# One PSUM bank, one more product in halves and two steps of delay in a gated mix of linear attention and a GEGLU network

## The chip, the cores and the metric

The kernel runs on one core of a Trainium2 chip. Its engines work beside each other and are kept in order by semaphores: TensorE (PE in the profile; its weight loads are PEld), VectorE (DVE), ScalarE (ACT), GpSimd (POOL) and SyncE (SP), whose queue issues most transfers. Matmuls write to PSUM, which has 8 banks of 512 float32 columns for each of 128 partitions. The metric is the device time of one execution in microseconds, as the median of several runs.

## The reference

The input x has 2048 tokens of 640 features (bfloat16). Two branches are computed from it and mixed by a gate for each token.

```python
def _A_ref(x, wqkv, w_phi, wo):          # linear attention, 32 heads of 20
    q, k, v = ...(x @ wqkv)
    pq = einsum("bhsd,hdf->bhsf", q, w_phi); pk = einsum("bhsd,hdf->bhsf", k, w_phi)
    phi_q = concatenate([softmax(pq), softmax(-pq)], axis=-1)
    phi_k = concatenate([softmax(pk), softmax(-pk)], axis=-1)
    kv = einsum("bhsf,bhsd->bhfd", phi_k, v); z = einsum("bhsf->bhf", phi_k)
    num = einsum("bhqf,bhfd->bhqd", phi_q, kv)
    den = einsum("bhqf,bhf->bhq", phi_q, z)[..., None] + 1e-6
    return (num / den) ... @ wo
def _B_ref(x, w_gate, w_up, w_down):     # F = 1728
    return (gelu(x @ w_gate) * (x @ w_up)) @ w_down
g = sigmoid((x * gate_w).sum(-1, keepdims=True))
out = g * _A_ref(x, ...) + (1 - g) * _B_ref(x, ...)
```

## The kernel before

Tokens are worked in 16 tiles of 128 and in 4 batches of 512. The order of all instructions is written out by hand. A small scheduler (`_Sched`) notes for each buffer key, such as a PSUM bank `("ps", b)`, who wrote and who read it last, and gives each new instruction the waits that follow. Every engine runs its instructions in that order, so an instruction that waits holds up all behind it on its engine.

The stages follow each other. `attention_state` (to about 81 us) projects keys, queries and values, takes exponentials on ScalarE, normalizes the key features on VectorE (`k_norm`, lines 617, 625 and 626) and sums the state tile by tile (`gram`, line 637). Then `ffn` runs. First come gate and up of the four batches, with 14 chunks of F columns each, in the order 0, 1, 13, 2, 3, ... 12. Then comes the down phase, one for each batch.

`gateup` (line 760) makes one chunk: 5 matmuls for the gate into the first bank of a pair, 5 for up into the second (line 464). ScalarE takes the gelu from the first bank (line 800), VectorE multiplies it with the second bank (line 803), in `gateup_evac`. The pairs take turns: banks (0, 1) and (6, 7) in batches 0 to 2, (2, 3) and (4, 5) in the first six chunks of batch 3. So chunks 0, 13 and 3 share a pair. Chunk 13 has only 64 gate and 64 up columns; both halves lie in one bank (`bk`), with 5 matmuls in all, one gelu (line 784) and two products (line 789). For chunks 2 to 6 of batch 0 the up half was computed ahead and lies in SBUF (`upheld`); there the pair is turned round, and the gate goes to what is otherwise the second bank. In batch 0 the last four tiles of the state (`gram(12)` to `gram(15)`) come after the first four chunks, and then `kv_state` and `gates` on VectorE.

The last eight chunks of batch 3 are made in groups of two by `gateup_halves` (line 806). It splits each matmul into two of 64 rows that run beside each other, one for a gate bank and one for an up bank (line 818). The groups hold chunks 5 and 6, 7 and 8, 9 and 10, 11 and 12, and use the banks (2, 3) and (4, 5), then twice (0, 1) and (6, 7), then (2, 3) and (4, 5). Before the first group stands numerator 0 in banks 0, 1, 6 and 7, before the third numerator 1 in banks 2 to 5. In the second group, chunk 7 is emptied in halves of 256 columns (`n=2` in `gateup_evac`: gelu of the first half, its product, gelu of the second half, its product), chunk 8 whole.

A numerator (`num`) is a set of 22 small matmuls (line 850) followed by eleven steps on VectorE (lines 868 to 881) and a transposing transfer on SP's queue into `goT` (line 884). In the down phase `down_pair` makes two token tiles at a time from `hT`, `goT` and the down and output weights (line 908), in banks 0, 1, 4 and 5; a batch has 148 steps of two matmuls, and after the steps listed in `at` comes a numerator for a later tile, always in banks 2, 3, 6 and 7. So each numerator waits until VectorE has read the one before out of these banks (line 879).

Of the kernel before, what the change touches and what calls it, by code (L numbers as in the profile page):

```python
# [107 lines left out]
class _Kernel:  # L108
# [651 lines left out]
    def gateup(self, b, c, banks):  # L760
        sc = self.sc
        xs = lambda kt: self.xT[:, kt, b * self.BT:(b + 1) * self.BT]
        xr = [("xT", t) for t in range(4 * b, 4 * b + 4)]
        old = (self.oldw, self.oldk, self.oldq, [("xT", t) for t in range(12)])[b]
        hT, hk = self.hT(b, c), b
        slot = self.gn % 3
        self.gn += 1
        if c < 13:
            i = 0 if c < 7 else 1
            early = c in self.UP + self.LATE  # L770
            done = early and b == 0
            if done:
                banks = banks[::-1]
            for w, wk, bk in ((self.wg_sb, "wg", banks[0]), (self.wu_sb, "wu", banks[1]))[:1 if done else 2]:
                for kt in range(self.KD):
                    key = self.upheld(c)[1] if early and wk == "wu" else (wk, i, kt)
                    self.mm(bk, 0, 512, w[:, kt, c * P:(c + 1) * P], xs(kt), kt == 0, kt == self.KD - 1, xr + [key])
            up, upk = (self.upheld(c)[0], ("upf", c)) if done else (self.bank(banks[1]), ("ps", banks[1]))
            self.gateup_evac(b, c, banks[0], slot, up, upk, old)
        else:  # L780
            bk = banks[0]
            for kt in range(self.KD):
                self.mm(bk, 0, 512, self.wgu_sb[:, kt, :], xs(kt), kt == 0, kt == self.KD - 1, xr + ["wgu0", "wgu1"])
            sc.op("act", lambda e: e.activation(self.gl[64:128, slot, :], self.ps[0:64, bk * 512:bk * 512 + 512],
                                                AF.Gelu_apprx_tanh),
                  reads=[("ps", bk)], writes=[("gl", slot)], guard=self.oldw)
            for r in (0, 1):
                odd = lambda v: v.rearrange("p (u r q) -> p u r q", r=2, q=P)[:, :, r, :]
                sc.op("dve", lambda e: e.tensor_tensor(
                    odd(hT[64 * r:64 * r + 64, :]), odd(self.ps[64:128, bk * 512:bk * 512 + 512]),  # L790
                    odd(self.gl[64:128, slot, :]), ALU.mult),
                    reads=[("ps", bk), ("gl", slot)], writes=[("hT", hk, c, r)], guard=old)
# [13 lines left out]
    def gateup_halves(self, b, cs, pairs, split):  # L806

        sc, KD = self.sc, self.KD
        old = [("xT", t) for t in range(12)]
        for close in (0, 1):  # L810
            for c, banks in zip(cs, pairs):
                i = 0 if c < 7 else 1
                for kt in range(KD):
                    for r in (0, 1):
                        w, wk, bk = ((self.wg_sb, "wg", banks[0]), (self.wu_sb, "wu", banks[1]))[r ^ close]
                        key = self.upheld(c)[1] if c in self.UP + self.LATE and wk == "wu" else (wk, i, kt)
                        a, end = 64 * r, kt == KD - 1
                        sc.op("pe", lambda e: e.matmul(  # L818
                            self.bank(bk), w[a:a + 64, kt, c * P:(c + 1) * P],
                            self.xT[a:a + 64, kt, b * self.BT:(b + 1) * self.BT], start=close == 0 and kt == 0,  # L820
                            stop=close == 1 and end, skip_group_check=True),
                            reads=[("xT", t) for t in range(4 * b, 4 * b + 4)] + [key],
                            writes=[("ps", bk)] + ([("turn", bk)] if end else []), signal=end,
                            after=[("turn", bk)] if close and kt == 0 else ())
                if close:
                    slot = self.gn % 3
                    self.gn += 1
                    self.gateup_evac(b, c, banks[0], slot, self.bank(banks[1]), ("ps", banks[1]), old,
                                     2 if split and c == cs[0] else 1)

    def before_num(self):
        return ([("upf", c) for c in self.UP + self.LATE] + ["kstage", "qstage"] + [("wref", k, h) for k in (0, 3) for h in (0, self.HM)] + [("wref", k, 0) for k in (1, 2, 4)] + [("xtok", k) for k in range(4)] + ["wkT", "wqT"])
# [125 lines left out]
    def ffn(self):  # L958
        self.gn = 0
        self.pn = 0  # L960
        pairs = [(0, 1), (6, 7)]

        order = [0, 1, 13] + list(range(2, 13))

        def gateups(b, after):
            for idx, c in enumerate(order):
                self.gateup(b, c, pairs[self.pn % 2])
                self.pn += 1
                after(idx)

        def downs(b, side):
            p = [(0, 1), (4, 5)]
            n = 0
            for t in (4 * b, 4 * b + 2):
                final = t + 2 == self.NT
                for _ in self.down_pair(t, p + [(2, 3)] if final else p, (256, 256, 128) if final else (320, 320)):
                    n += 1
                    if n in side:
                        self.num(side[n])

        def state(idx):
            if idx < 4:
                self.gram(12 + idx)
            if idx == 3:
                self.kv_state()
                self.gates()

        def none(idx):
            pass

        def last_gateups(b):
            middle, n = [(2, 3), (4, 5)], 6
            for idx in range(n):
                self.gateup(b, order[idx], middle[idx % 2])
            self.num(0, (0, 6))
            for g, banks in enumerate((middle, pairs, pairs, middle)):
                if g == 2:
                    self.num(1, (2, 4))
                self.gateup_halves(b, order[n + 2 * g:n + 2 * g + 2], banks, g == 1)
        at = [(5, 35, 65, 95)] + [(1, 31, 61, 91)] * 3  # L1000
        gateups(0, state)
        gateups(1, none)
        gateups(2, none)
        last_gateups(3)
        for b in range(self.NB):
            downs(b, {at[b][k]: 4 * b + 2 + k for k in range(4 if b < 3 else 2)})
# [44 lines left out]
```

## Time and profile before

| | |
|---|---|
| median of 3 runs | 283.40 us (283.25 to 283.69) |
| the profiled execution | 283.51 us, span 282.2 us |
| TensorE busy | 278.1 us (99% of the span) |
| VectorE, ScalarE busy | 173.3 us, 106.0 us |
| matmuls, weight loads | 2994, 3006 |
| batch 0 of gate and up begins | about 81 us |
| last batch's split groups | 176.84 to about 194.6 us |
| down phases | from about 194.3 us to the end |

The profile is one execution. Its rows give start and duration of instructions or of merged runs of them, what an engine was idle for, and which instruction released it. The chain is followed back from the last instruction, at each step to what released it.

### The profile page before, as it was taken

How to read it: one execution, taken by the hardware profiler on the slowest of the kernel's cores; microseconds unless marked ns; L12 is line 12 of the kernel's file. 1: busy time of each engine (PE TensorE's matmuls, PEld its weight loads, DVE VectorE, ACT ScalarE, POOL GpSimd, SP SyncE). 2: the span in 40 equal slices, each digit the busy share in tenths (PEclk: the TensorE clock that was granted, in tenths of full speed). 3: DMA queues.
4: the chain of work that ended last, by engine and by line, in shares of the span. 5: the costliest groups of instructions: out<-in, count | busy, mean ns of one | idle time of the engine just before them, and what ended most of it. 6: DMA issues, size and time to landing. Idle time of an engine off the chain costs nothing.

```text
span 282.2 us, 7054 instructions
## 1 busy us (share of the span) xinstructions
PE 278.1 (99%) x2994; PEld 186.2 (66%) x3006; DVE 173.3 (61%) x330; ACT 106.0 (38%) x205; POOL 15.1 (5%) x69
## 2 busy tenths in 40 slices
PE   8999999999999999999999999999999999999997
PEld 4576766666665444444444444456999999999996
DVE  2466999999997523333242233866984883883801
ACT  3347977877784332322323223122112112112011
POOL 7511001101000000000000000000000000000000
DMA  7999069787899910000000000101135132242221
GB/s 220 210 227 183 11 135 163 165 168 145 156 187 267 346 50 0 2 0 0 0 3 0 0 0 2 23 2 26 26 46 104 42 73 56 63 60 64 71 74 46
DMA packets 60378, 24.11 MB, mean 85 GB/s; under 512 B 51002, under 2 KB 59834, under 8 KB 60346
## 3 DMA queue, kind: packets, MB, share of 16 engines
q1 hardware_dynamic: 59680, 23.63, 39.1%
q8 instruction: 23, 0.38, 0.6%
q10 hardware_dynamic: 666, 0.03, 0.2%
q14 instruction: 9, 0.07, 0.1%
HBM read 9.04 MB, written 2.62 MB: 41 GB/s over the span
## 4 chain that ended last, share of the span: by engine, by line
PE 97%; DMA 1%; issue 0%; SPq 0%; ACT 0%
PE ps L464 52%; PE ps L908 29%; PE ps L818 6%; PE ps L599 4%; PE ps L478 2%; PE ps L850 2%; PE ps L637 2%; DMA xtok<-in_A_x_dram 1%; PE ps L404 1%; PE ps L342 0%; SPq L230 0%; ACT outsb L921 0%; PE ps L370 0%
## 5 line engine op out<-in xcount | busy, mean ns | idle before, releaser
L800 ACT ACTIVATE gl<-ps 128x512 bf16<-128x512 f32 (+1 forms) x53 | 31.1, 589 | 71.6 <-PE ps L464 57.0
L464 PE MATMUL ps<-xT,wu_sb 128*128 128x512 bf16 x214 | 52.9, 379 | 0.3
L464 PE MATMUL ps<-xT,wg_sb 128*128 128x512 bf16 x214 | 52.7, 379 | 0.3
L464 PE MATMUL ps<-w,xT 128*128 128x362 bf16 (+5 forms) x340 | 51.4, 302 | 0.0
L803 DVE TENSOR_TENSOR hT<-ps,gl 128x512 bf16<-128x512 f32 x34 | 23.4, 691 | 44.3 <-PE ps L464 44.3
L908 PE MATMUL ps<-wd_sb,hT 64*128 64x320 bf16 x648 | 49.5, 296 | 0.0
L908 PEld LDWEIGHTS ps<-wd_sb,hT 64*128 64x128 bf16 x648 | 40.8, 94 | 2.4
L464 PEld LDWEIGHTS ps<-w,xT 128*128 128x128 bf16 x340 | 31.9, 97 | 14.8
L921 ACT ACTIVATE outsb<-ps,Gm 128x320 bf16<-128x320 f32 (+2 forms) x31 | 14.5, 515 | 70.6 <-PE ps L908 70.6
L464 PEld LDWEIGHTS ps<-xT,wu_sb 128*128 128x128 bf16 x220 | 21.5, 98 | 25.6
L464 PEld LDWEIGHTS ps<-xT,wg_sb 128*128 128x128 bf16 x220 | 21.1, 98 | 25.4 <-ACT gl L800 0.4
L908 PE MATMUL ps<-wo_sb,goT 64*128 64x320 bf16 (+2 forms) x340 | 27.5, 288 | 0.0
L617 DVE TENSOR_REDUCE Dk<-Ek 128x66 f32<-128x1320 bf16 x16 | 24.3, 1521 | 2.3 <-ACT gcol L528 2.3
L626 DVE TENSOR_TENSOR Ek<-Ek,Dk 128x1320 bf16<-128x1320 bf16 x16 | 24.5, 1533 | 0.5
L879 DVE TENSOR_TENSOR O<-ps,RH 128x640 bf16<-128x640 f32 x32 | 24.8, 817 | 0.0
L538 ACT ACTIVATE Ek<-ps 128x627 bf16<-128x627 f32 x32 | 20.5, 693 | 6.4 <-PE ps L599 4.9
L538 ACT ACTIVATE Eqt<-ps 128x627 bf16<-128x627 f32 x32 | 20.6, 705 | 2.5 <-PE ps L464 2.5
L908 PEld LDWEIGHTS ps<-wo_sb,goT 64*128 64x128 bf16 x340 | 20.6, 94 | 1.0
L818 PE MATMUL ps<-xT,wg_sb 64*128 64x512 bf16 x80 | 17.7, 376 | 0.0
L818 PE MATMUL ps<-xT,wu_sb 64*128 64x512 bf16 x80 | 17.5, 376 | 0.0
L908 PE MATMUL ps<-wd_sb,xT 64*128 64x320 bf16 (+2 forms) x270 | 16.3, 269 | 0.0
L803 DVE TENSOR_TENSOR xT<-ps,gl 128x512 bf16<-128x512 f32 (+1 forms) x14 | 8.9, 651 | 11.9 <-PE ps L464 6.4
(94 smaller groups left out, 221.1 us busy)
## 6 DMA issues: line engine op xcount, KB each, us to landing
out_dram<-outsb SPq DMA_DIRECT2D x7, 320.0 KB, 3.2
wd_sb<-in_B_w_down_dram SPq DMA_DIRECT2D x1, 2080.0 KB, 10.9
wg_sb<-in_B_w_gate_dram SPq DMA_DIRECT2D x5, 224.0 KB, 3.1
wg_sb<-in_B_w_gate_dram SPq DMA_DIRECT2D x5, 192.0 KB, 3.1
wu_sb<-in_B_w_up_dram SPq DMA_DIRECT2D x5, 192.0 KB, 3.7
wo_sb<-in_A_wo_dram SPq DMA_DIRECT2D x1, 800.0 KB, 9.6
xtok<-in_A_x_dram SPq DMA_DIRECT2D x2, 320.0 KB, 3.3
w<-in_A_wqkv_dram SPq DMA_DIRECT2D x4, 160.0 KB, 3.6
```

The lines of the kernel that those rows point to most:

```text
L464: self.sc.op("pe", lambda e: e.matmul(self.ps[:, bank * 512 + c0:bank * 512 + c0 + n], lhs, rhs, start=first, stop=fin), reads=reads, writ ...
L478: sc.op("pe", lambda e, c0=c0, n=n, bk=bk, col=col: e.matmul(self.bank(bk)[:, col:col + n], self.xT[:, kt, t * P:(t + 1) * P], self.w3[:, ...
L538: self.sc.op("act", lambda e: e.activation(dst, src, AF.Exp, scale=scale), reads=[("ps", b), ("ps", b + 1)], writes=[(name, sl, s)])
L599: self.sc.op("pe", lambda e: e.matmul(out, self.xT[:, kt, t * P:(t + 1) * P], self.w3[:, kt, c:c + 2 * n].rearrange("p (r w) -> p r w", w= ...
L617: self.sc.op("dve", lambda e: e.tensor_reduce(self.Dk[:, se, 0, :].rearrange("p (u h) -> p u h", h=self.HG), self.k_view(se), AX.X, ALU.ad ...
L626: sc.op("dve", lambda e: e.tensor_tensor(v, v, R.rearrange("p (u h) -> p u h", h=self.HG).unsqueeze(3).to_broadcast([P, 2 * self.G, self.H ...
L800: sc.op("act", lambda e: e.activation(self.gl[:, slot, a:a + w], self.bank(bank)[:, a:a + w], AF.Gelu_apprx_tanh), reads=[("ps", bank)], w ...
L803: sc.op("dve", lambda e: e.tensor_tensor(hT[:, a:a + w], up[:, a:a + w], self.gl[:, slot, a:a + w], ALU.mult), reads=[upk, glk], writes=[( ...
L818: sc.op("pe", lambda e: e.matmul(self.bank(bk), w[a:a + 64, kt, c * P:(c + 1) * P], self.xT[a:a + 64, kt, b * self.BT:(b + 1) * self.BT], ...
L879: dve(lambda e, o=o, f=f, s=s: e.tensor_tensor(o, V[s][:, :, 0:DH], f, ALU.mult), rb[2 * s:2 * s + 2] + [key(6 + s)], [("O", s, sl)], guar ...
L908: sc.op("pe", lambda e: e.matmul(self.bank(bk, w), lhs, rhs, start=opens and x == 0, stop=end and not opens, skip_group_check=True), reads ...
L921: sc.op("act", lambda e: e.activation(dst, self.bank(bk, w), AF.Copy, scale=g), reads=rd, writes=wr)
```

## The change

Three edits. Chunk 13 of every batch goes to the second bank of its pair. In the second split group of batch 3 both chunks are emptied in halves, where it was only the first. In the down phase of batch 0 the numerators come after steps 5, 37, 67 and 97 instead of 5, 35, 65 and 95. The matmuls stay the same in number and size; one ScalarE and one VectorE instruction are added, since chunk 8's gelu and product become two each.

```diff
@@ gateup, chunk 13 @@
         else:
-            bk = banks[0]
+            bk = banks[1]
@@ gateup_halves @@
                     self.gateup_evac(b, c, banks[0], slot, self.bank(banks[1]), ("ps", banks[1]), old,
-                                     2 if split and c == cs[0] else 1)
+                                     2 if split else 1)
@@ ffn @@
-        at = [(5, 35, 65, 95)] + [(1, 31, 61, 91)] * 3
+        at = [(5, 37, 67, 97)] + [(1, 31, 61, 91)] * 3
```

## The prediction

> **What bounds the kernel now.** I read the page first: header, busy times, chain.
>
> ```profile
> span 282.2 us, 7054 instructions
> ...
> PE 278.1 (99%) x2994; PEld 186.2 (66%) x3006; DVE 173.3 (61%) x330; ACT 106.0 (38%) x205; POOL 15.1 (5%) x69
> ...
> PE 97%; DMA 1%; issue 0%; SPq 0%; ACT 0%
> ```
>
> TensorE is busy 278.1 of 282.2 us and carries 97% of the chain. Only two things can move the end: TensorE standing, or less work on it. The change touches no matmul's size or number, so all that counts is where TensorE stands. The list of waits, PEld rows, names who keeps it (the times include idle of the weight loader that costs nothing):
>
> ```profile
> PEld ps L464 <- ACT gl L800: 0.4, 1, 0.4
> ...
> PEld ps L818 <- DVE xT L803: 0.4, 1, 0.4
> PEld ps L850 <- DVE O L879: 0.2, 1, 0.2
> ```
>
> What each truly costs is read from the chain in order of time, since equal groups of matmuls should take equal time:
>
> ```profile
> 128.63 10.74 PE ps L464 x49
> 139.42 10.86 PE ps L464 x49
> 150.33 10.74 PE ps L464 x49
> ...
> 176.84 8.64 PE ps L818 x80
> 185.48 0.34 PE ps L850 x22
> 185.82 8.82 PE ps L818 x80
> ...
> 199.74 0.46 PE ps L850 x17
> ...
> 204.31 0.31 PE ps L850 x13
> ```
>
> The piece at 139.42 is 0.12 us longer than its neighbours, the second 80 split matmuls 0.18 us longer than the first, the numerator at 199.74 about 0.14 us longer than the next ones (0.31 to 0.33). These three lie exactly at what the three edits touch. All they can give back is some 0.4 us.
>
> **The change part by part.**
>
> *Chunk 13 in the second bank.* It takes the first pair's second bank, the one in which chunk 0's up product lay. ScalarE frees a first bank (gelu), VectorE the second (product), later. In batches 1 to 3 that product is long done (batch 1: it ends at 109.02, chunk 13 starts at 110.29), so chunk 13 pays nothing there. Chunk 3, the next in that pair, then finds its first bank free of chunk 13's two VectorE products, and its second bank is wanted only five matmuls later. Batch 2 shows what this saves: the products of L789 ran from 141.75 to 142.64 and chunk 3 started at 142.78, 0.34 us after the matmul before it instead of 0.22. **Gain 0.12 us.** In batches 1 and 3 the products were in time (113.14 for a start at 113.52; 171.53 for 171.92), so nothing is gained there. In batch 2 VectorE started them 0.46 us after the gelu (batch 1: 0.10), with no cause that I see; if that is chance and no habit, the gain is 0. I keep 0 to 0.12 and take 0.12.
>
> In batch 0 it is otherwise. VectorE is still normalizing key tile 15:
>
> ```profile
> 84.26 1.53 DVE L626 TENSOR_TENSOR Ek<-Ek,Dk 128x1320 bf16<-128x1320 bf16 x1
> ...
> 85.53 0.50 PE L637 MATMUL ps<-vaug,Ek 128*128 128x63 bf16 x11
> ...
> 85.71 0.68 DVE L803 TENSOR_TENSOR hT<-ps,gl 128x512 bf16<-128x512 f32 x1
> ...
> 85.84 0.34 PEld L464 LDWEIGHTS ps<-xT,wgu_sb 128*128 128x128 bf16 x3
> 85.87 0.59 PE L464 MATMUL ps<-xT,wgu_sb 128*128 128x512 bf16 x2
> ```
>
> The row at 85.71 is chunk 0's product; it ends at 86.39. Chunk 13's weight load now goes at 85.84, since bank 0 has been free since the gelu that ended at 84.30. In bank 1 it must wait for 86.39. From the end of a product to the weight load behind it the trace has two rows: 0.05 us (a product ends at 185.71, the load starts at 185.76) and 0.11 us (142.64 to 142.75). So the load starts at 86.44 to 86.50: **TensorE stands 0.60 to 0.66 us**, I take 0.63. Queued behind it on TensorE is everything: the tiles of the state (L637) at 86.94, chunk 2, the rest. Nothing later swallows it: after the first 6 us no transfer stands as releaser in TensorE's rows of the list of waits, and the matmuls follow each other closely.
>
> A second wait follows in the same batch. There chunk 3's up half was computed ahead, so its pair is turned round and its gate lies in bank 1, now behind chunk 13's products instead of chunk 0's. Both products move with chunk 13: today the second ends at 88.72, and chunk 3's first matmul is at 88.70. Add 0.05 to 0.11 us to the load and 0.03 from load to matmul: **0.10 to 0.16 us** more, I take 0.13. VectorE's work behind (KV state, gates, later products) moves with TensorE and kept no matmul waiting; ScalarE is idle for 0.48 us and more before each gelu of this stretch.
>
> *Both chunks ahead of the second numerator in halves.* The second group of the last batch (chunks 7, 8) is followed by numerator 1, and chunk 10 needs the second bank of chunk 8. Chunk 8 is now emptied whole: gelu from 185.55, product to 186.94; chunk 10's second stream starts at 186.99, though its rhythm (186.42, 186.64) would have put it at 186.86. Chunk 7, already in halves, is the row for the new form: first gelu at 184.47, second product ending at 185.71, 1.24 us against chunk 8's 1.39. So chunk 8's product would end at 185.55 + 1.24 = 186.79, the load follows by 186.84 and the matmul at 186.86. It just fits: **gain 0.13 us**; the other stream loses only 0.04 us today (186.74 to 187.00 instead of 0.216 later), so 0.04 is the low end. Two instructions are added, one on each of two engines, where each waits for the next matmuls anyway. The rows against it: two half gelus take 0.66 us and two half products 0.76 us, whole ones 0.60 and 0.69. The Trainium skill, "VectorE: DVE Perf Modes", section on the TRN2 errata, holds that each instruction pays a fixed latency once and advises tiles of 512 elements and more; by that rule alone the split gains nothing and the sum below would be 0.13 us larger. The row of chunk 7 decides against it here, because the two engines work on different halves at once.
>
> *Numerators at 5, 37, 67, 97.* Numerator 3 now meets VectorE still reading numerator 2's banks (L879 ends at 199.67; the load behind it starts at 199.72). A step is 4.11 us / 30 = 0.137 us, two are 0.27, so at step 37 it arrives 0.1 us after the release: **gain 0.14 us** (0.46 less 0.32); low end 0, if VectorE runs later than shown. Numerators 4 and 5 keep their distance of 30 steps. Each numerator's transposing DMA on SP goes 0.27 us later, and the output DMA queued behind numerator 4's with it; goT is read at least 65 steps, 9 us, later, and the output buffers not again in that batch.
>
> *Sum.* 0.63 + 0.13 − 0.12 − 0.13 − 0.14 = **+0.37 us**; best ends 0.60 + 0.10 − 0.12 − 0.13 − 0.14 = +0.31, worst 0.66 + 0.16 − 0 − 0.04 − 0 = +0.78. The profiled execution took 283.51 us (1.31 around its span) and would take 283.88. It lay 0.11 above the median of 283.40, which becomes **283.8**, from 283.7 to 284.2. What a measurement of this kernel can tell from no change is about 0.2%, 0.57 us: under 282.83 is faster, over 283.97 slower.
>
> **The rivals.**
>
> *VectorE sets the pace of the numerators (slower).* The numerator steps with their wait take VectorE from 200.39 to 204.01, and numerator 4's first matmul is at 204.12, one tenth of a microsecond after. If after the move numerators 4 and 5 meet VectorE later than now, the 0.13 and 0.14 come back as waits at L850: 0.63 + 0.13 − 0.12 = +0.64, 284.0. For: VectorE is 9 tenths busy in that slice of the page. Against: numerators from the fourth on take 0.31 to 0.33 us, no wait, at the same distance of 30 steps. It decides where a numerator's VectorE work outlasts 30 steps and the numerator's own matmuls, 4.4 us. Chance 0.20.
>
> *Chunk 0's product is in time (the batch 0 loss fails).* Then only the gains are left, −0.39: 283.0. VectorE would have to be 0.6 us earlier than shown, but it works without a pause from 78.49 to 86.99 us, and its lateness comes from the key tiles, which are not changed. Chance 0.10.
>
> *The pause slows TensorE's clock.* At the start the 512-column matmuls of L675 came 0.43 us apart, twice the later 0.216, for some 2.5 us; such a stretch again would add 1.25 us to the sum: 285.0. Against: the pause of 0.57 us at 4.53 (for xtok) was followed by L342 at the same pace as before, and the granted clock is 1.00 in all stages. Chance 0.04. The Trainium skill, "TensorE: Matmul & The Clock Gate", "A second HAM failure mode", tells of a kernel where short pauses between groups in cycled banks made the clock swing; nothing in this trace does so.
>
> **How the numbers follow.** Forecast 0.62, of it 0.48 within the bound and 0.14 beyond; VectorE's pace 0.20 (0.14 slower, 0.06 same); the missing loss 0.10 (0.07 same, 0.03 faster); the clock 0.04, slower; 0.04 for what I did not see, 0.01 of it faster, 0.03 slower. Slower 0.35, same 0.61, faster 0.04. The range runs from the 283.0 of the missing loss to 284.4, the worst ends (284.2) plus 0.2, half of the spread of the runs before (283.25 to 283.69); the clock case stays out.
>
> **What would show it.** Right: chunk 13's load in batch 0 starts about 0.6 us after the state's matmuls end, with VectorE's L803 as releaser; chunk 3's gate follows L789; the batch 2 piece is 10.74; the 80 split matmuls of the third and fourth group take some 8.7 us; the second numerator of down phase 0 takes 0.32. Wrong: no pause at 86 us, or pauses at the later numerators.

## The result and the profile after

The changed kernel takes 283.99 us as the median of 22 runs (283.73 to 284.62), the kernel before 283.56 us in 22 runs beside it (283.25 to 284.15). The ratio is 1.0016, with a 95% interval of 1.0010 to 1.0023: 0.43 us between the medians, small, but clear of zero; its centre is within the 0.2% bound that the prediction set. The profiled execution took 284.2 us.

The page of the changed kernel, header and busy times:

```profile
span 282.9 us, 7056 instructions
...
PE 278.8 (99%) x2994; PEld 189.6 (67%) x3006; DVE 173.4 (61%) x331; ACT 106.1 (38%) x206; POOL 15.2 (5%) x69
```

The same matmuls, one more instruction on VectorE and one on ScalarE, and a span 0.7 us longer. The list of waits, rows of the weight loader (total us, times, longest):

```profile
PEld ps L464 <- issue: 0.8, 2, 0.6
...
PEld ps L818 <- DVE xT L803: 0.2, 1, 0.2
```

Two rows of before are gone, that of ACT's L800 (it stood at chunk 3 of batch 2) and that of DVE's L879 (numerator 3). The L818 row has halved. In their place "issue" has a longest wait of 0.6 us instead of 0.2. What that is, the timeline shows around chunk 13 of batch 0 (start, duration, engine and line, count, and in brackets the idle time before and its releaser):

```profile
85.73 0.50 PE L637 MATMUL ps<-vaug,Ek 128*128 128x63 bf16 x11
85.91 1.28 DVE L803 TENSOR_TENSOR hT<-ps,gl 128x512 bf16<-128x512 f32 x2
...
86.71 0.34 PEld L464 LDWEIGHTS ps<-xT,wgu_sb 128*128 128x128 bf16 x3 [0.59 <-issue]
86.74 0.59 PE L464 MATMUL ps<-xT,wgu_sb 128*128 128x512 bf16 x2 [0.51 <-DVE hT L803]
```

The state's matmuls end, the first of the two products (chunk 0's) ends at 86.60, the weight load of chunk 13 goes 0.11 us later. The matmul's own row names L803. The chain in order of time has it as a piece of VectorE in the middle of TensorE's:

```profile
10.32 0.06 PE ps L370
...
83.73 2.18 PE ps L464 x10
85.91 0.69 DVE hT L803
86.60 0.14 issue
86.74 1.24 PE ps L464 x5
...
140.46 10.74 PE ps L464 x49
151.25 10.74 PE ps L464 x49
...
177.76 8.64 PE ps L818 x80
186.39 0.34 PE ps L850 x22
186.73 8.75 PE ps L818 x80
...
200.78 0.33 PE ps L850 x18
```

The piece of batch 2 is at 10.74 like its neighbours, the second 80 split matmuls take 8.75 instead of 8.82 us, numerator 3 takes 0.33 instead of 0.46.

Since both kernels have the same matmul groups in the same number, the two traces can be laid side by side: the completion signal of each matmul group, its time in the one less its time in the other. The difference stays level where TensorE flows in both, and steps where one of them stands. From the level after the first loads (L370) it steps by +0.66 at chunk 13 of batch 0, by +0.16 at chunk 3 of that batch, by −0.12 at chunk 3 of batch 2 and by −0.22 in all from chunk 10 to numerator 3. That is +0.48 us to the end. The other 0.21 us of the profile's 0.69 lie ahead of L370, which is at 10.32 instead of 10.12; the edits do not reach there.

### The profile page after: what moved, and what is told of

Its sections match the earlier page's. It is cut to its first block, busy times and chain, and to the rows that moved or that the text cites. A ratio compares the mean times of both kernels' runs of the same rounds, so it can differ in the third digit from the quotient of the medians.

```text
span 282.9 us, 7056 instructions
## 1 busy us (share of the span) xinstructions
PE 278.8 (99%) x2994; PEld 189.6 (67%) x3006; DVE 173.4 (61%) x331; ACT 106.1 (38%) x206; POOL 15.2 (5%) x69
## 4 chain that ended last, share of the span: by engine, by line
PE 98%; issue 0%; DVE 0%; ACT 0%
PE ps L464 52%; PE ps L908 28%; PE ps L818 6%; PE ps L599 4%; PE ps L850 2%; PE ps L478 2%; PE ps L637 2%; PE ps L675 1%; PE ps L404 1%; PE ps L342 0%; DVE hT L803 0%; ACT outsb L921 0%; PE ps L682 0%; PE ps L370 0%
## 5 line engine op out<-in xcount | busy, mean ns | idle before, releaser
L800 ACT ACTIVATE gl<-ps 128x512 bf16<-128x512 f32 (+1 forms) x54 | 31.2, 581 | 71.4 <-PE ps L464 57.1
L908 PE MATMUL ps<-wd_sb,hT 64*128 64x320 bf16 x648 | 51.1, 296 | 0.0
L803 DVE TENSOR_TENSOR hT<-ps,gl 128x512 bf16<-128x512 f32 x34 | 23.4, 692 | 44.2 <-PE ps L464 44.2
L908 PEld LDWEIGHTS ps<-wd_sb,hT 64*128 64x128 bf16 x648 | 42.4, 94 | 2.2
L908 PE MATMUL ps<-wo_sb,goT 64*128 64x320 bf16 (+2 forms) x340 | 29.3, 288 | 0.0
L879 DVE TENSOR_TENSOR O<-ps,RH 128x640 bf16<-128x640 f32 x32 | 24.8, 815 | 0.0
L908 PEld LDWEIGHTS ps<-wo_sb,goT 64*128 64x128 bf16 x340 | 22.2, 94 | 1.1
L818 PE MATMUL ps<-xT,wg_sb 64*128 64x512 bf16 x80 | 17.7, 376 | 0.0
L818 PE MATMUL ps<-xT,wu_sb 64*128 64x512 bf16 x80 | 17.5, 376 | 0.0
L803 DVE TENSOR_TENSOR xT<-ps,gl 128x512 bf16<-128x512 f32 (+1 forms) x15 | 9.0, 617 | 11.7 <-PE ps L464 6.4
```

Of the source, the lines that this page charges most:

```text
L800: sc.op("act", lambda e: e.activation(self.gl[:, slot, a:a + w], self.bank(bank)[:, a:a + w], AF.Gelu_apprx_tanh), reads=[("ps", bank)], w ...
L803: sc.op("dve", lambda e: e.tensor_tensor(hT[:, a:a + w], up[:, a:a + w], self.gl[:, slot, a:a + w], ALU.mult), reads=[upk, glk], writes=[( ...
L818: sc.op("pe", lambda e: e.matmul(self.bank(bk), w[a:a + 64, kt, c * P:(c + 1) * P], self.xT[a:a + 64, kt, b * self.BT:(b + 1) * self.BT], ...
L879: dve(lambda e, o=o, f=f, s=s: e.tensor_tensor(o, V[s][:, :, 0:DH], f, ALU.mult), rb[2 * s:2 * s + 2] + [key(6 + s)], [("O", s, sl)], guar ...
L908: sc.op("pe", lambda e: e.matmul(self.bank(bk, w), lhs, rhs, start=opens and x == 0, stop=end and not opens, skip_group_check=True), reads ...
```

## The experiments

The theory: the bank edit costs 0.66 + 0.16 us in batch 0, by two waits of TensorE on VectorE, and everything else is a small gain. The main rival: the later edits, halves and steps, load VectorE between 176 and 210 us and make the kernel longer. A second one: a bank that VectorE has just read costs its price in any order. Each ratio is against the kernel before on the same chip. It is worked out from the single runs of both kernels, not from the two medians (e1: 284.03 over 283.37 would be 1.0023).

**e1, the bank edit alone.**

```diff
 (before)
-            bk = banks[0]
+            bk = banks[1]
```

> The kernel before with chunk 13 in the second bank of its pair, in all four batches; the other two edits are left out. Theory (the waits on VectorE in batch 0 make the kernel longer): pauses of 0.66 us at chunk 13 and 0.16 us at chunk 3 in batch 0, 0.12 us less at chunk 3 of batch 2, so 0.70 us more than before, 1.0025 of it, and the last split groups and numerators as before. Rival (the later edits make it longer: halves and steps put more load on VectorE between 176 and 210 us): this kernel is 0.12 us shorter than before or the same, 0.9996 to 1.0000.

Measured: 284.03 us (before 283.37), ratio 1.0027, 1.0018 to 1.0036. Laid beside before, it steps by +0.66, +0.16 and −0.12 us at the same three places and then stays level: +0.72 at the end. The second 80 split matmuls take 8.82 us as before, and numerator 3 waits as before, as the chain shows:

```profile
86.11 0.69 DVE hT L803
...
186.93 8.82 PE ps L818 x80
...
200.86 0.46 PE ps L850 x17
```

By the traces the bank edit alone costs more than the whole change (+0.72 against +0.48; the intervals of the two ratios overlap). The main rival falls.

**e2, the two later edits alone.**

```diff
 (before)
-                                     2 if split and c == cs[0] else 1)
+                                     2 if split else 1)
...
-        at = [(5, 35, 65, 95)] + [(1, 31, 61, 91)] * 3
+        at = [(5, 37, 67, 97)] + [(1, 31, 61, 91)] * 3
```

> The kernel before with the two later edits (both chunks in halves, numerators at 5, 37, 67, 97), chunk 13 in the first bank as before. Theory: no pause in batch 0; 0.06 to 0.15 us less at chunk 10 and 0.09 to 0.15 us less at numerator 3, so 0.15 to 0.30 us less than before, 0.9990 to 0.9995; the wait of 0.12 us in batch 2 stays. Rival (VectorE's pace): 0.3 us or more above before, with waits at the numerators.

Measured: 283.23 us, ratio 0.9994, 0.9985 to 1.0003: the time alone cannot tell it from before. The trace can: no step in batch 0, then −0.21 us from chunk 10 to numerator 3, −0.20 at the end. Its chain has the wait of batch 2 that the bank edit removes, and the shorter pieces behind it:

```profile
139.92 10.87 PE ps L464 x49
150.84 10.74 PE ps L464 x49
...
186.33 8.75 PE ps L818 x80
...
200.38 0.33 PE ps L850 x18
```

**e3, the bank edit in batches 1 to 3 only, with the other two.**

```diff
 (changed)
-            bk = banks[1]
+            bk = banks[1] if b else banks[0]
```

> The changed kernel with chunk 13 of batch 0 back in the first bank, in the second bank in batches 1 to 3 only. Theory: both pauses in batch 0 go and all gains stay, so 0.83 us less than the changed kernel and 0.3 to 0.4 us less than before, 0.9986 to 0.9990. Rival (later edits): about as long as the changed kernel, 1.001 to 1.002. This is also the candidate to beat both kernels.

Measured: 283.04 us, ratio 0.9989, 0.9980 to 0.9997. Both steps in batch 0 are gone, the −0.12 of batch 2 and the −0.22 behind it stay: −0.34 us at the end. One condition on the batch turns the change from longer into shorter than before.

**e4, chunk 0's product ahead of the key tile's scaling.**

```diff
 (changed; attention_state, then state in ffn)
-                self.k_norm(nk)
+                self.k_sums(nk)
+                if nk < NT - 1:
+                    self.k_scale(nk)
...
         def state(idx):
+            if idx == 0:
+                self.k_scale(15)
```

> The changed kernel with one thing moved on VectorE: the scaling of key tile 15 (reciprocal and product, lines 625 and 626) stands behind chunk 0's product instead of ahead of it. Theory (what chunk 13 waits for is chunk 0's product, and that is late because of the key tile): chunk 0's product ends near 85.0 us, chunk 13 starts with no pause. The scaling then stands ahead of chunk 1's product, which ends near 87.75 us, and the turned pair makes chunk 2's gate wait for it, some 0.56 us; chunk 3's wait of 0.16 us goes, since chunk 13's products are done by then. In all 0.27 us less than the changed kernel: 1.0005 of before. Rival (a bank written after VectorE read it costs that much whatever VectorE's order): chunk 13's pause of 0.66 us stays and the time is that of the changed kernel, 1.0016, or more.

Measured: 283.39 us, ratio 0.9998, 0.9989 to 1.0007. The timeline (VectorE's rows first; the product is line 805 in this kernel):

```profile
84.31 0.69 DVE L805 TENSOR_TENSOR hT<-ps,gl 128x512 bf16<-128x512 f32 x1 [0.76 <-issue]
84.92 0.56 DVE L625 RECIPROCAL Dk<-Dk 128x66 f32<-128x66 f32 x1
85.51 1.53 DVE L626 TENSOR_TENSOR Ek<-Ek,Dk 128x1320 bf16<-128x1320 bf16 x1
...
86.96 0.68 DVE L805 TENSOR_TENSOR hT<-ps,gl 128x512 bf16<-128x512 f32 x1
...
85.79 1.24 PE L464 MATMUL ps<-xT,wgu_sb 128*128 128x512 bf16 x5
86.87 0.50 PE L637 MATMUL ps<-vaug,Ek 128*128 128x63 bf16 x11
87.93 0.59 PE L464 MATMUL ps<-xT,wg_sb 128*128 128x512 bf16 x2 [0.56 <-DVE hT L805]
```

Chunk 0's product ends at 85.00, and chunk 13 starts behind the state's matmuls without a pause, in the second bank. The pause has moved to chunk 2, whose gate waits for chunk 1's product (86.96 + 0.68 = 87.64, the matmul at 87.93). It is 0.50 us, against 0.56 expected, and chunk 3 waits for nothing: +0.18 us at the end, 0.30 less than the changed kernel, where 0.27 less was expected. So what chunk 13 paid for is the order on VectorE, not the bank as such.

**e5, the pairs of batch 0 not turned round.**

```diff
 (changed; gateup)
-            if done:
-                banks = banks[::-1]
```

> The changed kernel, but in batch 0 the pair of the chunks whose up half was computed ahead (2 to 6) is not turned round: their gates go to the first bank. Theory (chunk 3's gate waits 0.16 us because the turned pair puts it behind chunk 13's products): that wait goes, chunk 13's pause of 0.66 us stays; 0.16 us less than the changed kernel, 1.0011 of before. Rival (the second step of the delay belongs to the state's last tile or the KV work beside it): both steps stay, 1.0016.

Measured: 283.64 us, ratio 1.0013, 1.0004 to 1.0023. The intervals of this and the changed kernel overlap; the trace decides. It steps by +0.67 at chunk 13 and not at all at chunk 3: +0.32 us at the end, 0.16 less than the changed kernel. The second step was the turned pair.

**e6, both together.** The two edits of e4 and e5 on the changed kernel.

> The changed kernel with both: the scaling of key tile 15 behind chunk 0's product, and the pairs of batch 0 not turned. Theory: chunk 13 finds its bank free, chunk 2's and chunk 3's gates lie in first banks that the gelu frees; no pause is left in batch 0, though chunk 13 lies in the second bank in all four batches. So as long as the kernel with the bank changed in batches 1 to 3 only: 0.9989 of before. Rival (the second bank costs chunk 13 something in batch 0 in any order): between that and the changed kernel, 1.0005 or more.

Measured: 283.01 us, ratio 0.9985, 0.9977 to 0.9994. Chunk 13 lies in the second bank in all four batches, and batch 0 has no step left:

```profile
85.21 0.50 PE L637 MATMUL ps<-vaug,Ek 128*128 128x63 bf16 x11
85.27 1.53 DVE L626 TENSOR_TENSOR Ek<-Ek,Dk 128x1320 bf16<-128x1320 bf16 x1
...
85.55 1.24 PE L464 MATMUL ps<-xT,wgu_sb 128*128 128x512 bf16 x5
```

At the end −0.33 us, as e3. The second rival falls too.

**e7, e3 with numerator 2 after step 7.**

```diff
 (e3)
-        at = [(5, 37, 67, 97)] + [(1, 31, 61, 91)] * 3
+        at = [(7, 37, 67, 97)] + [(1, 31, 61, 91)] * 3
```

> The kernel with the bank changed in batches 1 to 3 only, and the first numerator of down phase 0 after step 7 instead of 5. Theory: it overwrites banks 2 and 3, which hold chunk 11 until its product ends about 0.05 us after numerator 2's first matmul; two steps later nothing is left to wait for, 0 to 0.1 us less than without this, 0.9986 to 0.9989 of before. Rival (VectorE's pace): numerator 3, now only 30 steps behind, meets VectorE late and 0.1 us or more comes back, 0.9992.

Measured: 283.23 us, ratio 0.9989, 0.9980 to 0.9998, and −0.33 us at the end of the trace: nothing gained on e3, nothing lost. The pieces of numerator 2 in the chain add up to 0.46 us in e1, where chunk 8 is emptied whole, to 0.40 in e3 and to 0.39 here, after step 7. So what was to be removed was gone in e3 already. Numerator 3, only 30 steps behind, takes 0.33 us and does not wait.

All kernels side by side, steps against before in us, from the traces:

| kernel | chunk 13, batch 0 | later in batch 0 | batch 2 | chunk 10 to the end | at the end | ratio measured |
|---|---|---|---|---|---|---|
| the change | +0.66 | +0.16 | −0.12 | −0.22 | +0.48 | 1.0016 |
| e1 bank alone | +0.66 | +0.16 | −0.12 | +0.02 | +0.72 | 1.0027 |
| e2 halves and steps | 0 | 0 | +0.01 | −0.21 | −0.20 | 0.9994 |
| e3 bank in 1 to 3 | 0 | 0 | −0.12 | −0.22 | −0.34 | 0.9989 |
| e4 late scaling | 0 | +0.50 | −0.12 | −0.20 | +0.18 | 0.9998 |
| e5 not turned | +0.67 | 0 | −0.12 | −0.23 | +0.32 | 1.0013 |
| e6 both | 0 | 0 | −0.12 | −0.21 | −0.33 | 0.9985 |
| e7 step 7 | 0 | 0 | −0.12 | −0.22 | −0.33 | 0.9989 |

## Why the prediction was right, point by point

The forecast was +0.37 us and 283.8 us; measured are 283.99 us, +0.43 between the medians and +0.48 in the traces. Most of what is missing to 283.99 is the start of the sum: it went out from 283.40, and the kernel before has 283.56 in its 22 runs. Every step lay where it was put. The terms for chunk 13, for chunk 3 and for the later edits were off by 0.03, 0.03 and 0.05 us, all the same way, so it is no luck of errors that cancel.

*Chunk 13 in batch 0:* 0.60 to 0.66 forecast, 0.66 found. The value taken, 0.63, lay between two rows for the time from a product's end to the load behind it, 0.05 and 0.11 us. Here it was 0.11 (86.60 to 86.71). In the trace an extra instruction that waits for semaphores stands ahead of this load (at 86.63), as ahead of the 0.11 row of before (at 142.68); ahead of the 0.05 row there is none.

*Chunk 3 in batch 0:* 0.10 to 0.16 forecast, 0.16 found, for the same reason: chunk 13's products end at 89.60, the load goes at 89.71. e5 shows that it is the turned pair.

```profile
88.71 0.89 DVE L789 TENSOR_TENSOR hT<-ps,gl 64x256 bf16<-64x256 f32 x2 [1.52 <-ACT gl L784]
...
89.71 0.77 PEld L464 LDWEIGHTS ps<-xT,wg_sb 128*128 128x128 bf16 x5
```

*Batch 2:* −0.12 forecast and found, in each kernel whose chunk 13 lies in the second bank there. The prediction left open whether VectorE's late start there was chance. It is habit: in all nine kernels the products start 0.46 to 0.47 us after the gelu in batch 2 and 0.10 us after it in the other three batches. Why is still open.

*Halves and steps:* −0.27 forecast, −0.22 found with all three edits, −0.21 in e2. The two gains together were over-sized by 0.05 us. Chunk 8's chain came out as worked from chunk 7's row: gelu from 186.46, second product to 186.95 + 0.76 = 187.71, 1.25 us against 1.39 whole, and chunk 10's second stream starts at 187.77, just on its rhythm.

```profile
187.56 0.38 PE L818 MATMUL ps<-xT,wu_sb 64*128 64x512 bf16 x1
187.65 0.38 PE L818 MATMUL ps<-xT,wg_sb 64*128 64x512 bf16 x1
187.77 0.38 PE L818 MATMUL ps<-xT,wu_sb 64*128 64x512 bf16 x1
187.87 0.38 PE L818 MATMUL ps<-xT,wg_sb 64*128 64x512 bf16 x1
```

But the two streams of half matmuls, which run beside each other, stay 0.1 us apart, as the rows show, where the wait of before had set them level. Laid beside before, the one stream gained 0.15 us, the other 0.06, and the stage's piece of the chain 0.07. From numerator 2 on, both streams of the down phase stand 0.15 us ahead. So this gain came in full; 0.13 had been taken.

What is missing lies at numerator 3. In the kernel before, VectorE releases both of its streams at once:

```profile
199.72 0.11 PEld L850 LDWEIGHTS ps<-KV,Eq 64*128 64x128 bf16 x4 [0.21 <-DVE O L879]
```

After the change it waits for nothing, for L879 is through at 200.43 and the first matmul starts at 200.59:

```profile
199.62 0.81 DVE L879 TENSOR_TENSOR O<-ps,RH 128x640 bf16<-128x640 f32 x1
...
200.59 0.52 PE L850 MATMUL ps<-KV,Eq 64*128 64x66 bf16 x19
```

Its streams now start 0.10 us apart (200.59 and 200.69), and so they stay. One gained 0.15 us more, the other 0.09, and the end of the kernel follows the other. The prediction had taken 0.14, the gain of the better stream, for the numerator as a whole. No run has the halves without the steps, so this split rests on where the steps lie in the traces.

The Trainium skill ("VectorE: DVE Perf Modes", the section on the TRN2 errata) holds, for operations that read SBUF, that many small tiles pay a fixed latency for each tile. The rows agree on the engine time, though the gelu reads PSUM alone and the product reads PSUM and SBUF (the halves take 0.66 and 0.76 us, the whole ones 0.60 and 0.69). They do not agree on what counts here, since the chain of two engines became shorter, 1.25 us instead of 1.39.

*The rivals.* VectorE's pace: e2 has the later edits alone, and numerators 3 to 5 take 0.32 to 0.33 us. The missing loss: e1 has it in full. The clock: behind the pause the pieces of 49 matmuls take 10.74 us as before, and the granted clock is 1.0. The pace is the better witness of the two, because the profile gives 1.00 for the first 3 us as well, where the matmuls of L675 come 0.43 us apart. The Trainium skill ("TensorE: Matmul & The Clock Gate", "A second HAM failure mode") tells of frequent short pauses between groups of matmuls that made the clock swing; the pause of 0.66 us here did not.

## What to carry to other kernels

A bank has two readers, and which of them is late differs from stage to stage: a swap that takes a wait away in the steady batches can put a longer one in the batch that starts while VectorE still works off the stage before, so each batch is costed by itself. Where TensorE is 99% busy, its pauses are found by comparing equal groups of matmuls, and two traces laid side by side show steps of 0.1 to 0.2 us, as in e2, that the times cannot tell from nothing. Two streams that run beside each other can gain differently when a wait goes, and the end may follow the one that gains less, as at numerator 3. When a wait is moved by a new order on another engine, look at once for who is next in that engine's queue: in e4 most of the pause reappeared one chunk later, at chunk 2.

## What the runs showed of the hardware that was not expected

The first 10 us differ between executions by more than the whole change. The small transpose of the gate column (L370) comes at 10.12 us in the profile of before, 10.32 in that of the changed kernel, 9.80 in e6 and 10.62 in e2, though all have the same work up to there. The chains of before and of e2 name the load of xtok as what came last, that of e6 the load of the value weights. Before, e2 and e6 in this order:

```profile
1.27 3.77 DMA xtok<-in_A_x_dram
5.09 0.47 PE ps L342 x20
5.56 4.56 PE ps L478 x36
10.12 0.06 PE ps L370
```

```profile
1.28 3.77 DMA xtok<-in_A_x_dram
...
5.09 0.71 PE ps L342 x20
5.81 4.81 PE ps L478 x36
10.62 0.06 PE ps L370
```

```profile
1.74 3.35 DMA w<-in_A_wqkv_dram
...
9.80 0.06 PE ps L370
```

In before and e2 this load ends at the same time, and yet they come out 0.50 us apart, so the load is not all of it. The same matmuls take longer in e2, 0.71 instead of 0.47 us and 4.81 instead of 4.56. In the traces TensorE's pace rises at a moment that differs between executions: at 4.0 us in before, 4.1 in e6, 6.2 in the changed kernel, 6.4 in e2 and 6.6 in e1. In the changed kernel, for instance, the matmuls of L478 come 0.18 us apart on average up to that moment and 0.09 behind it. What sets the moment no run here shows.

Everything behind is shifted by that much; where the edits do not reach, the traces then agree to about 0.01 us. So of the changed kernel's 0.69 us in the profile 0.21 are of this kind. That it also makes the spread of the unprofiled runs (283.25 to 284.15 for before) is likely, but no run here shows it.
